# Rotary products and low parts of q and k on GpSimd alone, softmax row sums from four tiles on TensorE, first q and k in one transfer

## The chip, the core and the metric

One core of a Trainium2 chip runs the whole program. The metric is the device time of one execution in microseconds (us). Before the change it is 661.58 us, the median of 3 runs (661.09 to 662.1). Engines are named as in the profile: PE is TensorE (PEld its weight loads), DVE is VectorE, ACT is ScalarE, POOL is GpSimd, SP is SyncE, which issues nearly all transfers.

## What is computed

Four batches of eight heads, 576 positions, 64 features a head. q and k are rotated by position (RoPE), attended with a softmax, and the result goes through a soft mixture of 8 experts and then a wide squared-ReLU layer. All inputs are float32; matmuls run on float32 operands, some of them split in a rounded high part and a low part.

```python
q_rot, k_rot = rotate(q), rotate(k)          # x1*cos - x2*sin, x1*sin + x2*cos
scores = matmul(q_rot, k_rot.T) / 8
attn = exp(scores - max(scores))
attn = attn / (sum(attn) + 1e-9)
x = matmul(attn, v)                          # to (2304, 512)
logits = x @ phi                             # 32 slots
slot_in = softmax(logits, axis=0).T @ x
slot_out[e] = relu(slot_in[e] @ w1[e]) @ w2[e]
x = softmax(logits, axis=1) @ slot_out
out = (relu(x @ w_in) ** 2) @ w_out
```

## The kernel before

The 32 heads are worked off as 16 pairs of heads, numbered 0 to 15; the two heads of a pair stand on partitions 0 to 63 and 64 to 127. For a pair p these things happen:

- `load` (L303) brings k, q and their copies with swapped halves, 1.18 MB, into one of two buffers (`raws[p % 2]`), by three transfers. The buffer is free for pair p + 2 when the low parts of pair p have been computed.
- `rope_pair` (L321) rotates in place: for k (t = 0) and for q (t = 1) three operations on tiles of 128 x 576, times cosine, times sine, and the sum. All of them go through the helper `tt`, L317.
- `parts_pair` (L341): ACT rounds the rotated tile to its high part (`hi`, L347, three buffers), and `lo = a - hi` is a fourth operation a tile (L352, through L317 too; its rows read tL<-arena,tE). A `hi` buffer is free when the scores of the pair three before are done.
- `max_unit` (L379), ten times: PE forms scores from the high parts (L388), DVE takes the maximum over 576 columns in PSUM (L395). `max_rows` (L399) turns the maxima into a row (L406, L411, L416), and two small transfers (L421) bring it to where PE reads it. This runs 14 units ahead of the scores.
- `st_unit` (L431), ten units a pair (two halves of the queries, five tiles of keys): PE forms the transposed scores (L440, L444), ACT the exponentials (L453) into a tile P, and POOL adds the P of keys 0 to 3 into one tile `acc` (L461, three additions a half). The P tiles are a ring of six, with two more for the fifth.
- `pv_unit` (L466): PE multiplies P with v (L474).
- `norm` (L478), once a half: PE sums `acc` and the fifth P over the keys by a matmul with ones (L489, two groups of 64 columns at a time), DVE transposes (L493), inverts (L499, L500), transposes back (L504) and scales the result (L509). Then the pair's logits (L528, L533, L540).

The scores, maxima, row sums and a few others share a ring of three PSUM slots. After pair 15 come the experts, fed by weights from HBM, and then the wide layer on PE (L1345).

The order on each engine is not written by hand. Every step is given to `Plan.op` with the engines it may run on and their assumed costs, a due time, and the data it reads and writes; `Plan.emit` then lists the steps by a model of when each engine, slot and datum comes free, and an engine executes its list strictly in that order. The due times count in units, ten to a pair. Engines with a choice are written as a table, as in

```python
EITHER = {"POOL": 1.6, "DVE": 0.95}
on = {0: {"DVE": 0.8}, 1: {"POOL": 1.45}}.get(p, EITHER)
```

Transfers stand on SP in one list as well: the rows of maxima, v, the three of `load`, the expert weights.

## Time and profile before

| | |
|---|---|
| median of 3 runs | 661.58 us (661.09 to 662.1) |
| the profiled execution | 661.12 us, of which the trace spans 659.3 |
| mean granted TensorE clock | 0.968 |
| busy over the span: PE, DVE, ACT, POOL | 602.9, 438.4, 279.8, 256.3 us |
| last addition of logits (end of attention) | starts at 360.32 us |
| first matmul of L1345 on the chain (wide layer) | 425.79 us |

The span falls into three stages. Up to about 361 us the 16 pairs are worked off; POOL computes only here. From there to about 425 us the experts run while the weights stream in. From there to the end the wide layer keeps PE busy. A time in the rows below is counted from the span's start; "idle before" is the time an engine stood still before an instruction, and the name behind it is what ended that wait.

### The profile page before, as it was taken

The numbers are of one execution on the slowest core, as the hardware profiler recorded it, in microseconds if no ns is written. First come the engines' busy times: TensorE is split into PE (matmuls) and PEld (weight loads), VectorE is DVE, ScalarE is ACT, GpSimd is POOL, SyncE is SP. The second block draws the span as 40 slices with busy tenths as digits, with TensorE's granted clock in tenths as the row PEclk, the third lists the DMA queues.
The fourth block names the chain that finished last, engine by engine and source line by source line (L and its number), as shares of the span: only waits on it lengthen the run. The fifth ranks groups of instructions, "written<-read, shape, count | busy, mean of one in ns | idle before, by whom it ended". The sixth has DMA issues, their size and how long they took to land.

```text
span 659.3 us, 11254 instructions
## 1 busy us (share of the span) xinstructions
PE 602.9 (91%) x4437; PEld 408.2 (62%) x4437; DVE 438.4 (66%) x744; ACT 279.8 (42%) x492; POOL 256.3 (39%) x178
## 2 busy tenths in 40 slices
PE   2798998989889899899998988999999999999996
PEld 2555565546556555565665432677788788778885
DVE  2799867867776888776643543598569458455543
ACT  1142443434333444335443132479585446443440
POOL 1988988769666787666452000000000000000000
PEclk9688998998889999999999999999999999999999
DMA  8475534664365313402324999842130011000222
GB/s 183 95 169 157 152 106 121 157 156 128 93 157 156 83 30 76 93 21 85 136 79 157 390 387 389 338 127 82 47 128 1 0 65 64 1 1 0 96 95 96
DMA packets 36452, 80.76 MB, mean 122 GB/s; under 512 B 7632, under 2 KB 8048, under 8 KB 35440
## 3 DMA queue, kind: packets, MB, share of 16 engines
q1 hardware_dynamic: 35536, 79.16, 40.2%
q10 hardware_dynamic: 864, 0.89, 0.7%
q8 instruction: 35, 0.57, 0.4%
q14 instruction: 17, 0.14, 0.1%
HBM read 75.24 MB, written 4.72 MB: 121 GB/s over the span
## 4 chain that ended last, share of the span: by engine, by line
PE 55%; DMA 17%; DVE 9%; POOL 9%; issue 4%; SPq 3%; ACT 2%; DVEq 0%; POOLq 0%; ACTq 0%
PE bank L1345 30%; DMA arena<-in_qk_dram 13%; PE bank L474 5%; PE bank L440 4%; POOL arena L317 4%; DVE arena L317 4%; POOL pb L461 3%; PE bank L1277 2%; POOL tL L317 2%; PE bank L489 2%; SPq L309 2%; DVE mcol L395 2%; DMA pb<-in_w_in_dram 2%; PE bank L1071 2%; PE bank L1131 2%
## 5 line engine op out<-in xcount | busy, mean ns | idle before, releaser
L453 ACT ACTIVATE tO<-bank 128x576 f32<-128x576 f32 (+1 forms) x160 | 100.7, 648 | 187.5 <-PE bank L444 167.8
L1345 PE MATMUL bank<-w,tE 128*128 128x512 f32 x648 | 162.5, 399 | 1.1 <-ACT w__897 L1360 1.1
L1345 PEld LDWEIGHTS bank<-w,tE 128*128 128x128 f32 x648 | 120.6, 188 | 30.0 <-issue 2.9
L395 DVE TENSOR_REDUCE mcol<-bank 128x2 f32<-128x576 f32 x160 | 115.0, 745 | 34.3 <-PE bank L388 34.3
L474 PE MATMUL bank<-tO,pb 128*64 128x288 f32 x640 | 108.2, 436 | 2.6 <-DVE pb L509 2.4
L461 POOL TENSOR_TENSOR pb<-pb,tO 128x576 f32<-128x576 f32 x64 | 96.4, 1507 | 11.6 <-ACT tO L453 9.5
L317 POOL TENSOR_TENSOR arena<-arena 128x576 f32<-128x576 f32 x51 | 82.8, 1636 | 34.1 <-DMA arena<-in_qk_dram 30.2
L317 DVE TENSOR_TENSOR arena<-arena 128x576 f32<-128x576 f32 x45 | 64.3, 1444 | 21.2 <-DMA arena<-in_qk_dram 10.5
L440 PE MATMUL bank<-tE 64*128 64x288 f32 x320 | 60.5, 375 | 8.2 <-DVE mcol L395 6.2
L388 PE MATMUL bank<-tE 64*128 64x288 f32 x320 | 50.4, 352 | 17.4 <-DVE mrow L416 10.4
L461 POOL TENSOR_TENSOR pb<-tO 128x576 f32<-128x576 f32 x32 | 51.0, 1593 | 36.7 <-ACT tO L453 36.7
L440 PEld LDWEIGHTS bank<-tE 64*128 64x128 f32 x320 | 31.6, 194 | 46.3 <-issue 12.1
L474 PEld LDWEIGHTS bank<-tO,pb 128*64 128x64 f32 x640 | 35.5, 138 | 31.9 <-issue 17.4
L388 PEld LDWEIGHTS bank<-tE 64*128 64x128 f32 x320 | 29.9, 198 | 38.8 <-DVE mrow L416 12.9
L1345 PE MATMUL bank<-w,tO 128*128 128x512 f32 x216 | 52.7, 395 | 0.0
L440 PE MATMUL bank<-tL,tE 64*128 64x288 f32 x320 | 49.3, 305 | 0.0
L440 PE MATMUL bank<-tE,tL 64*128 64x288 f32 x320 | 49.2, 304 | 0.0
L444 PE MATMUL bank<-tE,pick 64*128 64x288 f32 x320 | 49.1, 303 | 0.0
L1345 PEld LDWEIGHTS bank<-w,tO 128*128 128x128 f32 x216 | 40.4, 188 | 8.8
L1288 ACT ACTIVATE pb<-bank 128x384 f32<-128x384 f32 x48 | 22.0, 493 | 49.5 <-PE bank L1277 36.1
L1288 ACT ACTIVATE arena<-bank 128x384 f32<-128x384 f32 x48 | 21.6, 489 | 35.1 <-PE bank L1277 33.4
L493 DVE STREAM_TRANSPOSE bank<-bank 128x288 f32<-128x288 f32 x32 | 15.8, 494 | 29.4 <-PE bank L489 29.4
(245 smaller groups left out, 840.1 us busy)
## 6 DMA issues: line engine op xcount, KB each, us to landing
arena<-in_qk_dram SPq DMA_DIRECT2D x15, 576.0 KB
arena<-in_qk_dram SPq DMA_DIRECT2D x15, 512.0 KB
pb<-in_v_dram SPq DMA_DIRECT2D x16, 320.0 KB
arena<-in_w_dram SPq DMA_DIRECT2D x8, 512.0 KB
tE<-in_w_dram SPq DMA_DIRECT2D x8, 512.0 KB
tL<-in_w_in_dram SPq DMA_DIRECT2D x3, 1024.0 KB
pb<-in_w_in_dram SPq DMA_DIRECT2D x3, 1024.0 KB
w__429<-in_w_dram SPq DMA_DIRECT2D x4, 512.0 KB
```

The lines of the kernel that those rows point to most:

```text
L309: lambda rows=rows, to=to, of=of, q=q: QUEUE[q].dma_start(out=raws[i][rows, ts_, to], in_=qk[p][rows, ts_, of]),
L317: ENG[e].tensor_tensor(out=o, in0=x, in1=y, op=how)
L388: nc.tensor.matmul(on_ring(tok)[:, j, 0:HQ], lhsT=hi[rows, 1, UNIT[u]], rhs=hi[rows, 0, HALF[h]], start=True, stop=True)
L395: lambda e: nc.vector.tensor_reduce(out=mcol[:, h, :, u], in_=on_ring(tok)[:, :, 0:HQ], op=ALU.max, axis=AX.X),
L440: nc.tensor.matmul(st[:, j, 0:HQ], lhsT=k[x][rows, UNIT[u]], rhs=q[y][rows, HALF[h]], start=(i == 0), stop=False)
L444: nc.tensor.matmul(st[:, j, 0:HQ], lhsT=pick[rows, :], rhs=mrow[rows, HALF[h]], start=False, stop=True)
L453: lambda e: nc.scalar.activation(out=pr[0:m], in_=on_ring(tok)[0:m, :, 0:HQ], func=AF.Exp, scale=0.125),
L461: lambda e: nc.gpsimd.tensor_tensor(out=acc, in0=one, in1=pr, op=ALU.add),
L474: nc.tensor.matmul(o_t[rows, 0:HQ], lhsT=vr[:, u, j, :], rhs=pr[:, j, :], start=(u == 0), stop=(u == 4))
L493: {"DVE": 0.47}, lambda e: nc.vector.transpose(out=on_ring(tok)[:, 1, 0:HQ], in_=on_ring(tok)[:, 0, 0:HQ]),
L1288: lambda e, i=i, h=h: nc.scalar.activation(out=rg_of()[:, 0, h], in_=BANKS[i][:, 0:384], func=AF.Relu),
L1345: nc.tensor.matmul(BANKS[PO[c]], lhsT=gt[:, x, 128 * c : 128 * c + 128], rhs=wo[:, fc % 2, y, :], start=(fc % FQ == 0 and i == 0), stop=(f ...
```

## The change

- `rope_pair`: all pairs but the first are rotated on POOL alone; before, pair 1 was, and the others could go to either engine.
- `parts_pair`: all low parts are formed on POOL alone; before, only those of pair 0.
- `st_unit`: POOL adds one pair of P tiles a half (keys 0 and 1), where it made three additions.
- `norm`: PE sums four things, `acc` and the P tiles of keys 2, 3 and 4, by eight matmuls of 32 columns of ones in four column groups; each group holds half of a head's sum. `inverse` gets four small additions (32 x 9) that add the partner group's half before the reciprocal.
- `first_loads`: the k and q of pair 0 come by one group of three transfers ahead of the tables, where two groups stood around the tables.
- the due times of the maxima of pair 1 are not below 0.1 + 0.4 n.

```diff
@@ rope_pair
-        on = {0: {"DVE": 0.8}, 1: {"POOL": 1.45}}.get(p, EITHER)
+        on = {"POOL": 1.45} if p else {"DVE": 0.8}
@@ parts_pair
-                EITHER if p else {"POOL": 1.45}, lambda e, a=a, hi=hi, lo=lo: tt(e, lo, a, f(hi), ALU.subtract), g + 2 * t + 1,
+                {"POOL": 1.45}, lambda e, a=a, hi=hi, lo=lo: tt(e, lo, a, f(hi), ALU.subtract), g + 2 * t + 1,
@@ st_unit
-        if 0 < u < 4:
-            one, k1 = p_slot(p, h, 0) if u == 1 else (acc, ak)
+        if u == 1:
+            one, k1 = p_slot(p, h, 0)
@@ norm
-        acc, (rest, rk) = accs[n], p_slot(p, h, 4)
+        acc, rest = accs[n], [p_slot(p, h, u) for u in (2, 3, 4)]
         tok = {}
+        QUAD = [slice(32 * i, 32 * i + 32) for i in range(4)]
 
         def sums(e):
             sm = on_ring(tok)[:, 0]
-            for i, x in enumerate((acc, rest)):
-                for j, rows in enumerate(HEADS):
-                    nc.tensor.matmul(sm[rows, 0:HQ], lhsT=ones, rhs=x[:, j, :], start=(i == 0), stop=(i == 1))
-
-        op({"PE": 1.1}, sums, g, [("acc", n), rk], [("sm", n)], take="ring", tok=tok, mode="c")
+            xs_ = [acc] + [x for x, _ in rest]
+            for i in range(2):
+                for j in range(2):
+                    for w in range(2):
+                        nc.tensor.matmul(
+                            sm[QUAD[2 * j + w], 0:HQ], lhsT=ones[:, 0:32], rhs=xs_[2 * i + w][:, j, :], start=(i == 0), stop=(i == 1)
+                        )
+
+        op({"PE": 1.15}, sums, g, [("acc", n)] + [k for _, k in rest], [("sm", n)], take="ring", tok=tok, mode="q")
@@ norm, inverse
             nc.vector.tensor_scalar(out=r9, in0=col, scalar1=1e-9, scalar2=None, op0=ALU.add)
+            for q in range(4):
+                nc.vector.tensor_tensor(out=r9[QUAD[q]], in0=r9[QUAD[q]], in1=col[QUAD[q ^ 1]], op=ALU.add)
             nc.vector.reciprocal(out=r9, in_=r9)
-        ring_op({"DVE": 0.39}, inverse, g, [("sm", n)], ["r9"], give="ring", tok=tok)
+        ring_op({"DVE": 0.9}, inverse, g, [("sm", n)], ["r9"], give="ring", tok=tok)
@@ first_loads
-        load(0, -99, slice(0, 4, 2), "ACT")
+        load(0, -99, slice(0, 4), "ACT")
...
-        load(0, -98.8, slice(1, 4, 2), "ACT")
@@ the loop over pairs
-            at(gm + n, max_unit, p, n // 2, n % 2, gm + n + (0.9 if n % 2 else 0.1))
+            at(gm + n, max_unit, p, n // 2, n % 2, max(gm + n + (0.9 if n % 2 else 0.1), 0.1 + 0.4 * n if p == 1 else -99))
```

The new lines shift the numbers: L474 stays, L489 becomes L492, L528 becomes L535.

Since the plan decides the order, three places of it follow, as the built programs have them.

POOL in the steady stretch, from the low parts of one pair to those of the next. Rows arena<-arena are rotary operations, tL<-arena,tE low parts, pb the additions of P tiles. Before, from the low parts of pair 12 to that of pair 13 (the other half of the operations stands on DVE):

```order
L317 TENSOR_TENSOR tL<-arena,tE 128x576 x2
L461 TENSOR_TENSOR pb<-tO_78 128x576
L461 TENSOR_TENSOR pb<-pb,tO_79 128x576 x2
L317 TENSOR_TENSOR arena<-arena 128x576 x2
L461 TENSOR_TENSOR pb<-tO_78 128x576
L317 TENSOR_TENSOR arena<-arena 128x576
L461 TENSOR_TENSOR pb<-pb,tO_78 128x576 x2
L317 TENSOR_TENSOR tL<-arena,tE 128x576
```

With the change, from the low parts of pair 13 to those of pair 14. The row "arena x2" is k of pair 15 times cosine and sine, whose data come by the load that waits for the low parts of pair 13; the addition after it is that of pair 11, second half:

```order
L317 TENSOR_TENSOR tL<-arena,tE 128x576 x2
L317 TENSOR_TENSOR arena<-arena 128x576
L461 TENSOR_TENSOR pb<-tO_79 128x576
L317 TENSOR_TENSOR arena<-arena 128x576 x2
L461 TENSOR_TENSOR pb<-tO_78 128x576
L317 TENSOR_TENSOR arena<-arena 128x576 x3
L317 TENSOR_TENSOR tL<-arena,tE 128x576 x2
```

All of the rotation now stands between one pair's low parts and the next's, and one addition stands behind the first two of its operations.

PE around the row sums of pair 11, second half, in pair 12. Before:

```order
L474 MATMUL bank_87<-tO_78,pb 64x288 x2
L489 MATMUL bank_86<-pb,ones 64x288 x2
L489 MATMUL bank_86<-tO_79,ones 64x288 x2
L388 MATMUL bank_85<-tE 128x288 x2
L440 MATMUL bank_84<-tE 128x288 x2
```

With the change:

```order
L474 MATMUL bank_87<-tO_78,pb 64x288 x2
L492 MATMUL bank_85<-pb,ones 32x288
L492 MATMUL bank_85<-tO_79,ones 32x288
L492 MATMUL bank_85<-pb,ones 32x288
L492 MATMUL bank_85<-tO_79,ones 32x288 x5
L388 MATMUL bank_84<-tE 128x288 x2
L440 MATMUL bank_86<-tE 128x288 x2
```

The sums stand at the same place among their neighbours, behind the fourth unit of pair 12, with eight narrow matmuls for four wide ones.

ACT at the start, where it issues transfers beside SP. Before:

```order
L309 DMA arena<-in_qk_dram 64x2x512
L309 DMA arena<-in_qk_dram 64x2x64
L818 DMA arena<-in_rope_dram 64x2x512
L818 DMA arena<-in_rope_dram 64x2x64
L309 DMA arena<-in_qk_dram 64x2x512
L309 DMA arena<-in_qk_dram 64x2x64
```

With the change:

```order
L309 DMA arena<-in_qk_dram 64x4x512
L309 DMA arena<-in_qk_dram 64x4x64
L825 DMA arena<-in_rope_dram 64x2x512
L825 DMA arena<-in_rope_dram 64x2x64
L347 ACTIVATE tE<-arena 128x576 x4
```

The second group behind the tables is gone; its bytes stand in the first.

## Rows read from the trace of the kernel before

**Rows 1.** The page, span in 40 equal slices: TensorE's granted clock in tenths of full speed

```profile
PEclk9688998998889999999999999999999999999999
```

**Rows 2.** Windows: steady stretch; one pair after the rotations end (us, busy PE, PEld, DVE, ACT, POOL, clock)

```profile
54.00:296.40 242.40, 220.84 (x2098) 137.42 (x2100) 189.61 (x322) 96.35 (x172) 187.65 (x121) 0.95 0.45 115
...
316.30:333.70 17.40, 17.40 (x180) 11.10 (x180) 11.06 (x24) 7.01 (x12) 8.50 (x6) 1.00 0.57 201
```

**Rows 3.** Waits of PE in 54 to 296 us: total us, times, longest

```profile
PE bank L388 <- DVE mrow L416: 10.4, 7, 3.0
PE bank L440 <- DVE mcol L395: 5.8, 6, 1.8
```

**Rows 4.** Groups of instructions: count, busy us, mean ns, idle before and its causes

```profile
L461 POOL TENSOR_TENSOR pb<-pb,tO 128x576 f32<-128x576 f32 x64 | 96.4, 1507 | 11.6 <-ACT tO L453 9.5
...
L317 POOL TENSOR_TENSOR arena<-arena 128x576 f32<-128x576 f32 x51 | 82.8, 1636 | 34.1 <-DMA arena<-in_qk_dram 30.2 <-DVE m L406 3.6
...
L317 DVE TENSOR_TENSOR arena<-arena 128x576 f32<-128x576 f32 x45 | 64.3, 1444 | 21.2 <-DMA arena<-in_qk_dram 10.5 <-DMA arena<-in_rope_dram 8.1 <-issue 2.5
...
L317 POOL TENSOR_TENSOR tL<-arena,tE 128x576 fp32r<-128x576 f32 x17 | 25.9, 1529 | 16.4 <-DMA arena<-in_qk_dram 14.3 <-ACT tE L347 1.9 <-PE bank L489 0.3
...
L317 DVE TENSOR_TENSOR tL<-arena,tE 128x576 fp32r<-128x576 f32 x15 | 20.6, 1378 | 2.3 <-ACT tE L347 2.3
```

**Rows 5.** Timeline of POOL (start, us, instruction): beside a DVE rotation; after the rotations

```profile
60.76 1.92 POOL L461 TENSOR_TENSOR pb<-pb,tO 128x576 f32<-128x576 f32 x1
...
321.51 1.41 POOL L461 TENSOR_TENSOR pb<-pb,tO 128x576 f32<-128x576 f32 x1 [0.20 <-ACT tO L453]
```

**Rows 6.** Timeline of POOL: low parts, then the first rotation on the next load

```profile
156.84 2.80 POOL L317 TENSOR_TENSOR tL<-arena,tE 128x576 fp32r<-128x576 f32 x2 [0.28 <-PE bank L489]
...
169.87 3.86 POOL L317 TENSOR_TENSOR arena<-arena 128x576 f32<-128x576 f32 x2 [4.99 <-DMA arena<-in_qk_dram]
...
243.23 2.79 POOL L317 TENSOR_TENSOR tL<-arena,tE 128x576 fp32r<-128x576 f32 x2
...
254.86 3.88 POOL L317 TENSOR_TENSOR arena<-arena 128x576 f32<-128x576 f32 x2 [3.64 <-DMA arena<-in_qk_dram]
...
265.20 1.41 POOL L317 TENSOR_TENSOR tL<-arena,tE 128x576 fp32r<-128x576 f32 x1
...
275.88 3.88 POOL L317 TENSOR_TENSOR arena<-arena 128x576 f32<-128x576 f32 x2 [4.18 <-DMA arena<-in_qk_dram]
```

**Rows 7.** The chain that ended last: the load is issued

```profile
266.64 0.55 SPq L309
```

**Rows 8.** Timelines at the start: DVE, POOL, PE

```profile
10.93 1.43 DVE L317 TENSOR_TENSOR arena<-arena 128x576 f32<-128x576 f32 x2 [8.08 <-DMA arena<-in_rope_dram]
14.83 2.89 DVE L317 TENSOR_TENSOR arena<-arena 128x576 f32<-128x576 f32 x4 [2.47 <-issue]
...
17.11 3.23 POOL L317 TENSOR_TENSOR tL<-arena,tE 128x576 fp32r<-128x576 f32 x2 [14.31 <-DMA arena<-in_qk_dram]
...
31.93 0.61 PE L440 MATMUL bank<-tE 64*128 64x288 f32 x2
```

**Rows 9.** Timeline of POOL: low part of pair 5

```profile
95.06 1.40 POOL L317 TENSOR_TENSOR tL<-arena,tE 128x576 fp32r<-128x576 f32 x1
```

**Rows 10.** Timelines: PE, sums of pair 11's second half; DVE, last logits

```profile
291.08 0.66 PE L489 MATMUL bank<-pb,ones 128*64 128x288 f32 x4
...
292.15 0.40 PE L388 MATMUL bank<-tE 64*128 64x288 f32 x2
...
360.32 0.35 DVE L540 TENSOR_TENSOR lg<-lg,bank 128x192 f32<-128x192 f32 x1 [0.70 <-PE bank L533]
```

**Rows 11.** Timeline of PE: matmuls in four groups of 32 columns; groups: a small DVE operation

```profile
363.13 1.42 PE L634 MATMUL bank<-x,es 128*32 128x512 f32 x16 [0.38 <-DVE es L601]
...
L499 DVE TENSOR_SCALAR r<-bank 128x9 f32<-128x9 f32 x32 | 4.8, 151 | 0.1
```

**Rows 12.** Windows: experts (us, busy PE, PEld, DVE, ACT, POOL, clock, DMA share, GB/s)

```profile
360.00:380.00 20.00, 18.46 (x153) 9.16 (x149) 9.82 (x42) 5.15 (x16) 0.53 (x1) 1.00 1.04 386
```

## The prediction

> **What bounds the kernel now.** I read the windows first. In the steady stretch of the 16 pairs, 54 to 296 us, PE is busy for 220.8 of 242.4 us, and the clock granted to it averages 0.95 [rows 2]; in slices up to 200 us it is below nine tenths of full speed, so part of them ran at 1.2 instead of 2.4 GHz, and after 200 us no slice is [rows 1]. The reader is to compare this with the second window: once the rotations are over, a whole pair takes 17.4 us with PE busy in all of it at full clock, while DVE and POOL do little [rows 2]. So PE has 21.6 us of idle time and 0.05 x 242.4 = 12.1 us of lost clock that are not its own work. The waits of PE say whose they are: the two rows on DVE (the row of maxima, and single maxima, that come late) hold 16.2 of the 21.6 us [rows 3]. DVE is late because its list holds rotations: 45 of them at 1.44 us and 15 low parts at 1.38 us, with idle time in front of them that transfers end [rows 4]. A rotation that waits for its data holds up every maximum listed behind it.
>
> I then followed POOL from pair to pair, because the change puts the rest there. The reader is to see a loop in it: low parts end, the freed buffer is loaded, POOL stands until the load has landed, rotates, and forms the next low parts. From the end of the low parts to the first rotation on the new data it takes 169.87 - 159.64 = 10.2, 254.86 - 246.02 = 8.8 and 275.88 - 266.61 = 9.3 us [rows 6]; SP issues the load 0.03 us after the low part ends [rows 7], so the rest is the transfer.
>
> **The change, part by part.**
>
> *DVE.* It loses 39 rotations (45 less the 6 of pair 0) and 15 low parts: 39 x 1.44 + 15 x 1.38 = 77 us, all of it ahead of maxima that PE waits for. It gains 4 x 32 small additions. No row shows one of 32 x 9; between nothing and the 151 ns of the nearest row, of 128 x 9 from PSUM [rows 11], I take 0.15, so 0.6 us a half and 19 us in all. DVE was busy for 189.6 of 242.4 us [rows 2] and will be for less, so this hides, but for the last half, where the end waits for it: +0.6 us.
>
> *POOL.* It loses 64 additions, 64 x 1.51 = 96 us, and gains 54 operations. What one costs depends on DVE: beside a DVE rotation 1.92 us, without one 1.41 us, although DVE then was busy with maxima, transposes and scaling for 11 of 17.4 us [rows 2, 5]. DVE keeps only operations of the second kind after pair 0, so I take 1.40 for each; the other end is 1.92.
>
> First the row, then two rules. POOL takes 1.4 us where a DVE rotation that meets no POOL operation takes 1.43 / 2 = 0.72 us [rows 5, 8]. The Trainium skill (GPSIMD Engine Reference, Engine selection) says elementwise work belongs on VectorE, since a two-input operation is about twice as slow on GpSimd. By that rule 54 moved operations cost 54 x (1.40 - 0.72) = 37 us of engine time, and the sum below would be some 37 us higher if POOL were the path throughout; by the rows POOL is on the path in part of the loop only. The Trainium skill (SBUF — State Buffer, Who interferes with whom) has a DVE operation with two SBUF inputs and a GpSimd operation that reads SBUF exclude each other for a whole instruction. That would make a contended one 1.40 + 0.72 = 2.1 us, and the trace has 1.92; with the change it leaves POOL uncontended.
>
> *The loop.* With the change a pass of it holds, behind the load, six operations (five rotations and one addition) and two low parts; the sixth rotation and the other addition run during the load. That is 9.3 + 8 x 1.40 = 20.5 us a pass, with 9.3 the middle of the three waits above. It is longer than PE's 17.4 us [rows 2], so **the loop, not PE, sets the pace** from pair 6 to 13. Of its eight passes (low parts of pair 5 to those of 13) the program's list has one with an operation less and one with one more: 6 x 20.5 + 19.1 + 21.9 = 164.0 us.
>
> *The start.* The first rotations wait for the tables until 10.93, the second group of pair 0 comes at 14.83, because it shares the queues with pair 1, and the six rotations end at 17.72 [rows 8]. In one transfer ahead of the tables, the whole of pair 0 has landed when the tables have. At about 10.9 six rotations of 0.72 end at 15.2: -2.5 us. Nothing gained, if the tables behind the larger transfer come at 13.4, is the other end; I take -2.5, as the bytes ahead of pair 1 are the same.
>
> *Up to pair 5.* POOL starts at 17.11 and ends the low part of pair 5 at 96.46 [rows 8, 9]. With the change it holds 51 operations there, 51 x 1.40 = 71 us, or 86 us from an earlier start of 14.6, if it never waits; it will wait for the loads of pairs 3 to 6, each of which follows the low parts by 9.3. I take the time of before less the start, 94.0, between 86 and 100.
>
> *PE.* The sums hold twice the instructions. Before, eight take 292.15 - 291.08 = 1.07 us, two groups at a time [rows 10]. If four groups run at a time, sixteen take the same; if only two do, 1 us more. Sixteen of mostly 512 columns in four groups take 1.42 us [rows 11], which only fits four at a time. I take +0.1 for the narrower steps and the change of grouping beside the P x v matmuls; before the end nine sums lie on the path: +0.9 us. In the loop's stretch PE waits anyway.
>
> *The sum.* The low parts of pair 13 end at 94.0 + 164.0 = 258.0. The load takes 9.3; two rotations and the second addition of pair 11 end 4.2 later, at 271.5. The sums of that half are listed behind the fourth unit of pair 12 and need that addition. Before, they started at 291.08 [rows 10]. So 271.5 - 291.1 = -19.6 us, and from there to the last logits at 360.32 [rows 10] the work is PE's as before. With +0.9 and +0.6: -18.1 us. The experts run under transfers at 386 GB/s [rows 12] that start as attention's buffers come free, and the wide layer follows; both move with it. 661.1 - 18.1 = **643 us** against the profiled execution's 661.12, which is 0.46 below the median of 661.58.
>
> What is late next: PE before the row sums, on POOL's addition, and then ACT, which must write the high parts of a pair in its list's order and has the exponentials queued behind them.
>
> **The rivals.**
>
> *PE bounds throughout.* If loads land sooner (SP issues them earlier, nothing else being late) the loop has slack, and all of PE's idle time and clock come back: 21.6 + 12.1 + 2.5 - 1.5 = 34.7 us, **626 us**. For it: the window at 17.4 us a pair. Against: none of the three waits is under 8.8 us, and even that gives 20.0 a pass.
>
> *The loop is longer.* With the longest wait seen, 10.2, nine waits make it 8 us later, and the early passes up to 4: **651 to 655 us**. For it: the expert weights load in the same stretch. Still faster.
>
> *POOL stays contended and the change loses.* Between the low parts of pair 5 and the sums of pair 11's second half stand 67 POOL operations on the path. At 1.92 instead of 1.40 they take 35 us more: **678 us**. The point from which it decides: 18.1 / 67 = 0.27, so at a mean over 1.67 us the change is slower. For it: the mean of POOL's rotations now is 1.64 [rows 4], just below. Against: that mean comes with DVE rotations, and the additions after these end take 1.41 [rows 5].
>
> *The wait only changes its name.* The loop now runs at 20.6 us (266.61 - 246.02) [rows 6]. If PE waits for POOL in the end as long as it did for DVE, the time is **660 to 662**. Against: it would need the slack that the loop already shows against PE's end to vanish.
>
> **How the numbers follow.** The forecast has 0.61, the longer loop 0.20, PE as the bound 0.09, the same time 0.03, the contended POOL 0.07. A measurement of this kernel tells about 0.2% from no change. Faster is 0.61 + 0.20 + 0.09 = 0.90, same 0.03, slower 0.07. The forecast's own bounds are a wait of 8.8 (nine of them: -4.5) and pair 5 at 86 (-8) on one side, pair 5 at 100 (+6) and no gain at the start (+2.5) on the other, which seldom fall together: 634 to 651. With the longer loop the range goes to 655; PE as the bound, the same time and the contended POOL are left out (0.19): 634 to 655.
>
> **What would show it.** POOL's rotations at a mean near 1.40 us, and no DVE rows of L317 but six. First score matmul at about 28 to 29.5 instead of 31.93. Low parts of pair 13 near 258. PE's waits: the row of maxima nearly gone, in its place the row sums (L492) on POOL's addition, or ACT's high parts on POOL. The span between the sums of pair 11 and the last logits stays about 69 us. It is wrong if POOL's mean stays over 1.6, if DVE still ends PE's longest waits, if sixteen narrow matmuls take over 1.5 us, or if PE is busy all through 150 to 270 us.

## The result, and the profile after

The changed kernel takes 641.92 us (median of 4 runs, 641.52 to 642.19) beside 661.84 us for the kernel before on the same chip: a ratio of 0.9687, with a 95% interval of 0.965 to 0.9725. It is faster. 643 had been forecast, and the range of 634 to 655 holds the time. The profiled execution took 642.19 us and spans 640.4.

The sum came out within 2 us, but the way it was reached did not. The signs that the prediction named separate the two, so I take them first from the profile.

The page of the kernel after, costliest groups (line, engine, operation, count | busy us, mean ns of one | idle time just before them and what ended it); they answer to [rows 4]:

```profile
L317 POOL TENSOR_TENSOR arena<-arena 128x576 f32<-128x576 f32 x90 | 125.4, 1414 | 56.3 <-DMA arena<-in_qk_dram 56.0
L461 POOL TENSOR_TENSOR pb<-tO 128x576 f32<-128x576 f32 x32 | 45.2, 1413 | 39.6 <-ACT tO L453 39.6
L317 POOL TENSOR_TENSOR tL<-arena,tE 128x576 fp32r<-128x576 f32 x32 | 45.2, 1427 | 20.6 <-ACT tE L347 20.6
L506 DVE TENSOR_TENSOR r<-r,bank 32x9 f32<-32x9 f32 x128 | 20.7, 162 | 2.4
```

POOL's operations take 1.41 to 1.43 us, as forecast, where rotations took 1.64 before. The small additions take 0.162 us (0.15 was assumed).

The windows of both kernels over equal work, from the logits of pair 0 to those of pair 12. The columns are the stretch, its length, the busy time of PE, of its weight loads, of DVE, ACT and POOL (with instruction counts), the granted clock, and the share and rate of the DMA engines. First the kernel before:

```profile
65.21:316.25 251.04, 229.74 (x2192) 141.64 (x2192) 192.46 (x334) 101.99 (x187) 188.40 (x122) 0.96 0.42 106
```

and the kernel after, with its last stretch to the last logits behind it:

```profile
63.14:295.17 232.03, 221.93 (x2384) 132.38 (x2384) 153.24 (x387) 101.34 (x188) 164.66 (x120) 1.00 0.47 120
295.17:342.06 46.89, 42.69 (x474) 26.07 (x473) 23.25 (x71) 16.99 (x30) 7.29 (x7) 0.99 0.36 127
```

The twelve pairs are 251.04 - 232.03 = 19.0 us shorter. PE's idle time falls from 251.04 - 229.74 = 21.3 to 10.1 us, which gives 11.2; the other 7.8 us is PE's busy time, which shrinks although PE now has more instructions, because the granted clock rises from 0.96 to 1.00. Behind pair 12 it goes the other way: 46.89 us to the last logits, where before it took 360.32 - 316.25 = 44.1 us.

The waits of PE from 30 to 345 us (operation <- what released it: us in total, times, longest), which answer to [rows 3]:

```profile
PE bank L474 <- DVE pb L516: 11.0, 23, 0.6
PE bank L535 <- DVE pb L516: 2.7, 1, 2.7
PE bank L474 <- DMA pb<-in_v_dram: 0.9, 1, 0.9
PE bank L492 <- DVE mcol L395: 0.7, 1, 0.7
```

The waits for the row of maxima and for single maxima, 16.2 us before, are gone. In their place is one of half a microsecond, 23 times in the 32 halves: P x v (L474) waits for the scaling on DVE (L516). There is no row at all in which PE waits for POOL. That contradicts the step of the prediction in which POOL's loop sets the pace.

Two timelines show that wait. The first is DVE in the kernel after, behind the row sums of one half (start, us, instruction, idle before it):

```profile
244.10 0.50 DVE L498 STREAM_TRANSPOSE bank<-bank 128x288 f32<-128x288 f32 x1 [1.08 <-PE bank L492]
244.51 0.72 DVE L395 TENSOR_REDUCE mcol<-bank 128x2 f32<-128x576 f32 x1
245.15 0.15 DVE L504 TENSOR_SCALAR r<-bank 128x9 f32<-128x9 f32 x1
245.34 0.69 DVE L506 TENSOR_TENSOR r<-r,bank 32x9 f32<-32x9 f32 x4
246.06 0.21 DVE L507 RECIPROCAL r<-r 128x9 f32<-128x9 f32 x1
246.31 0.48 DVE L511 STREAM_TRANSPOSE pb<-r 128x288 f32<-128x288 f32 x1
246.89 0.46 DVE L516 TENSOR_TENSOR pb<-bank,pb 128x288 f32<-128x288 f32 x1
```

The second is PE in the same stretch:

```profile
246.51 0.42 PE L388 MATMUL bank<-tE 64*128 64x288 f32 x4
247.41 0.71 PE L474 MATMUL bank<-tO,pb 128*64 128x288 f32 x4 [0.48 <-DVE pb L516]
```

The four small additions stand in this chain with 246.06 - 245.34 = 0.72 us. PE runs out of other work 0.48 us before the chain ends.

POOL in the same kernel, over one pass of its loop:

```profile
251.79 2.78 POOL L317 TENSOR_TENSOR tL<-arena,tE 128x576 fp32r<-128x576 f32 x2
254.54 1.39 POOL L317 TENSOR_TENSOR arena<-arena 128x576 f32<-128x576 f32 x1
255.90 1.41 POOL L461 TENSOR_TENSOR pb<-tO 128x576 f32<-128x576 f32 x1
262.80 2.79 POOL L317 TENSOR_TENSOR arena<-arena 128x576 f32<-128x576 f32 x2 [5.49 <-DMA arena<-in_qk_dram]
265.55 1.40 POOL L461 TENSOR_TENSOR pb<-tO 128x576 f32<-128x576 f32 x1
266.91 4.17 POOL L317 TENSOR_TENSOR arena<-arena 128x576 f32<-128x576 f32 x3
271.04 2.77 POOL L317 TENSOR_TENSOR tL<-arena,tE 128x576 fp32r<-128x576 f32 x2
```

The low parts of pair 13 end at 254.57 (258.0 was forecast), and the addition that pair 11's second row sums need ends at 266.95. Those sums start 1.9 us later:

```profile
268.89 0.43 PE L492 MATMUL bank<-pb,ones 128*32 128x288 f32 x1
```

This pass takes 271.04 - 251.79 = 19.3 us. The eight passes from pair 5 (its low parts end at 93.81) to pair 13 take (254.57 - 93.81) / 8 = 20.1 us in the mean, and PE's pairs over the same stretch (313.99 - 160.40) / 8 = 19.2, from logits to logits. So the loop is even the longer of the two, and yet PE does not wait for it, because POOL starts with a lead. Its addition for the second half of pair 4 is this one:

```profile
124.80 1.42 POOL L461 TENSOR_TENSOR pb<-tO 128x576 f32<-128x576 f32 x1
```

It ends 9.4 us before the sums that need it, which start at 135.66. For the second halves of pairs 7, 9 and 11 the lead is 4.6, 3.5 and 1.9 us. The rotations are over before it is used up.

### The profile page after: what moved, and what is told of

It reads as the page before. It is cut to its first block, busy times and chain, and to the rows that moved or that the text cites. A ratio compares the mean times of both kernels' runs of the same rounds, so it can differ in the third digit from the quotient of the medians.

```text
span 640.4 us, 11744 instructions
## 1 busy us (share of the span) xinstructions
PE 593.0 (93%) x4689; PEld 396.3 (62%) x4689; DVE 386.6 (60%) x818; ACT 278.6 (43%) x492; POOL 215.6 (34%) x168
## 4 chain that ended last, share of the span: by engine, by line
PE 76%; DVE 14%; DMA 5%; issue 2%; ACT 2%; SPq 1%; DVEq 0%; ACTq 0%
PE bank L1351 31%; PE bank L474 11%; PE bank L440 9%; PE bank L492 6%; DVE mcol L395 4%; PE bank L388 3%; PE bank L1283 3%; DVE r L506 2%; DMA pb<-in_w_in_dram 2%; PE bank L444 2%; DMA arena<-in_rope_dram 2%; PE bank L1077 2%; DVE pb L516 2%; PE bank L558 2%; DVE pb L511 2%
## 5 line engine op out<-in xcount | busy, mean ns | idle before, releaser
L317 POOL TENSOR_TENSOR arena<-arena 128x576 f32<-128x576 f32 x90 | 125.4, 1414 | 56.3 <-DMA arena<-in_qk_dram 56.0
L474 PE MATMUL bank<-tO,pb 128*64 128x288 f32 x640 | 105.0, 426 | 11.9 <-DVE pb L516 11.0
L474 PEld LDWEIGHTS bank<-tO,pb 128*64 128x64 f32 x640 | 34.9, 135 | 42.1 <-DVE pb L516 16.3
L461 POOL TENSOR_TENSOR pb<-tO 128x576 f32<-128x576 f32 x32 | 45.2, 1413 | 39.6 <-ACT tO L453 39.6
L440 PE MATMUL bank<-tE 64*128 64x288 f32 x320 | 56.7, 351 | 0.1
L317 POOL TENSOR_TENSOR tL<-arena,tE 128x576 fp32r<-128x576 f32 x32 | 45.2, 1427 | 20.6 <-ACT tE L347 20.6
L388 PE MATMUL bank<-tE 64*128 64x288 f32 x320 | 49.3, 341 | 2.5 <-DVE mcol L395 1.6
L440 PEld LDWEIGHTS bank<-tE 64*128 64x128 f32 x320 | 30.1, 185 | 31.6 <-issue 21.3
L440 PE MATMUL bank<-tL,tE 64*128 64x288 f32 x320 | 47.2, 292 | 0.0
L444 PE MATMUL bank<-tE,pick 64*128 64x288 f32 x320 | 47.2, 291 | 0.0
L440 PE MATMUL bank<-tE,tL 64*128 64x288 f32 x320 | 47.2, 291 | 0.0
L388 PEld LDWEIGHTS bank<-tE 64*128 64x128 f32 x320 | 28.6, 188 | 24.4 <-issue 10.8
L492 PE MATMUL bank<-tO,ones 128*32 128x288 f32 x384 | 37.5, 410 | 0.0
```

Of the source, the lines that this page charges most:

```text
L317: ENG[e].tensor_tensor(out=o, in0=x, in1=y, op=how)
L388: nc.tensor.matmul(on_ring(tok)[:, j, 0:HQ], lhsT=hi[rows, 1, UNIT[u]], rhs=hi[rows, 0, HALF[h]], start=True, stop=True)
L440: nc.tensor.matmul(st[:, j, 0:HQ], lhsT=k[x][rows, UNIT[u]], rhs=q[y][rows, HALF[h]], start=(i == 0), stop=False)
L444: nc.tensor.matmul(st[:, j, 0:HQ], lhsT=pick[rows, :], rhs=mrow[rows, HALF[h]], start=False, stop=True)
L461: lambda e: nc.gpsimd.tensor_tensor(out=acc, in0=one, in1=pr, op=ALU.add),
L474: nc.tensor.matmul(o_t[rows, 0:HQ], lhsT=vr[:, u, j, :], rhs=pr[:, j, :], start=(u == 0), stop=(u == 4))
```

## The experiments

The theories, as the expectations name them. **A** is the prediction's: POOL's loop sets the pace. **B**: PE and the DVE chain behind its row sums do, with POOL's loop about 2 us behind. **C**: as B, but the loop has all the slack it needs. The second batch gave rise to **D**, on what exactly PE waits for. The kernel before measured 661.1 to 664.9 us in these batches, so kernels of different batches are compared through their ratios to it.

| run | median us | ratio to before | 95% interval |
|---|---|---|---|
| the change | 641.92 | 0.9687 | 0.965 to 0.9725 |
| small additions left out | 638.94 | 0.9661 | 0.9619 to 0.9702 |
| POOL's addition left out | 641.18 | 0.9694 | 0.9658 to 0.9731 |
| both left out | 628.24 | 0.9496 | 0.9453 to 0.954 |
| rotations on either engine again | 669.16 | 1.0129 | 1.0062 to 1.0196 |
| old row sums | 639.74 | 0.9689 | 0.9651 to 0.9726 |
| first q and k in two groups | 640.11 | 0.9692 | 0.9653 to 0.9731 |
| row sums earlier | 645.51 | 0.9774 | 0.9735 to 0.9813 |
| row sums earlier, load split | 646.36 | 0.9794 | 0.9748 to 0.9839 |
| row sums earlier, two output tiles | 634.14 | 0.9547 | 0.9494 to 0.9601 |
| the same, load split | 638.29 | 0.9596 | 0.9556 to 0.9636 |
| row sums earlier, two output tiles, first q and k in two groups | 631.13 | 0.952 | 0.9502 to 0.9538 |
| two output tiles alone | 638.72 | 0.9637 | 0.9618 to 0.9656 |

### Who sets the pace: two additions, each left out, and both

The first edit takes the small additions out of the chain:

```diff
             nc.vector.tensor_scalar(out=r9, in0=col, scalar1=1e-9, scalar2=None, op0=ALU.add)
-            for q in range(4):
-                nc.vector.tensor_tensor(out=r9[QUAD[q]], in0=r9[QUAD[q]], in1=col[QUAD[q ^ 1]], op=ALU.add)
             nc.vector.reciprocal(out=r9, in_=r9)
```

> The four small additions of each half (32 x 9, between the row sums and the reciprocal) are left out, their place in the lists kept; each row sum then holds half of its terms. Theory A, the prediction's (POOL's loop of load, rotations and low parts sets the pace, the small additions hide behind it but for the last half): 641.9 - 0.6 = 641.3, between 640.5 and 642. Theory B (PE sets the pace, and the chain on DVE after the row sums holds up the first P x v of every half by some 0.5 us; POOL's loop stands only about 2 us behind): from pair 0 to 11 the loop takes over after 2 us are gained, and the 9 halves behind it give 9 x 0.5: 641.9 - 2 - 4.5 = 635.4, between 633 and 637. Theory C (as B, but POOL's loop has all the slack it needs): 32 x 0.5 = 16 us less, 626, between 624 and 629.

The second takes the addition off POOL:

```diff
-                lambda e: nc.gpsimd.tensor_tensor(out=acc, in0=one, in1=pr, op=ALU.add),
+                lambda e: None,
...
-            xs_ = [acc] + [x for x, _ in rest]
+            xs_ = [rest[0][0]] + [x for x, _ in rest]
```

> POOL's addition of the first two tiles of each half (32 x 1.40 us) is left out, the lists else the same; the row sums take the third tile twice in its place, so the sums lack two of five tiles. Theory A (POOL's loop sets the pace): a pass loses 2 x 1.4 = 2.8 us, over the eight passes 22 us, until PE bounds: 620 to 627. Theories B and C (PE and the chain behind its row sums set the pace): the two additions a pass were not on the path, 641 to 642.

The third has both edits.

> Both left out: the small additions on DVE and POOL's addition of two tiles, so the row sums lack most of their terms. Theory A: as without POOL's addition alone, 620 to 627, and no more than 1 us below that run. Theory B: POOL's loop falls to about 17.5 us a pass and stands behind no longer, so all 32 halves give their 0.5 us: 625 to 628, some 8 to 10 us below the run without the small additions alone. Theory C: the same as without the small additions alone, within 1 us.

Measured: 641.18 without POOL's addition (A wanted 620 to 627), 638.94 without the small additions, and 628.24 without either; B's ranges for these two end 2 us and 0.2 us lower. Leaving the small additions out gives 0.26% of the time of before while POOL has its additions (within the intervals), and 0.9694 - 0.9496 = 2.0%, or 13 us, once POOL has none. Such a pair of numbers is what two limits close to each other look like: either one, removed alone, uncovers the other.

**A falls.** Without its additions POOL only stands longer. The waits of POOL in that run, from 54 to 272 us, where the kernel after has 54.5 us for the same transfers:

```profile
POOL arena L317 <- DMA arena<-in_qk_dram: 74.0, 12, 9.7
```

B's second half also shows, by a path that no theory had named. In the run without the small additions the waits of PE from 30 to 345 us begin:

```profile
PE bank L444 <- DMA tE<-mrow: 6.5, 3, 3.6
```

PE waits for the row of maxima, that is for a transfer of 3 KB. SyncE's queue in the same run says why:

```profile
154.39 1.87 SPq L309 DMA_DIRECT2D arena<-in_qk_dram  x3
156.30 1.07 SPq L802 DMA_DIRECT2D w__1594<-in_w_dram  x2
157.47 1.50 SPq L421 DMA_DIRECT2D tE<-mrow  x2
```

The load of a pair (L309) is issued when POOL's low parts end, at 154.36. The expert weights and then the row stand behind it in the list. The row is issued at 157.47 and PE can use it at 166.18, after the 1.18 MB of the load and 1 MB of weights ahead of it. So a late low part on POOL reaches PE through the queue, and PE does not need to wait for POOL itself. With POOL's additions left out as well, that load is issued at 150.04 and the row at 156.74, and no such wait is left in PE's list.

The same place shows what such a pause costs besides its length. Windows of that run, with the columns as above:

```profile
162.00:166.10 4.10, 0.59 (x8) 0.36 (x6) 1.89 (x5) 0.00 (x0) 2.27 (x2) 0.91 0.72 232
166.10:168.00 1.90, 1.82 (x8) 1.09 (x10) 0.00 (x0) 0.65 (x1) 1.90 (x3) 0.50 0.00 0
168.00:170.00 2.00, 2.00 (x14) 1.14 (x12) 0.46 (x1) 0.00 (x0) 2.00 (x2) 0.50 0.00 0
170.00:172.00 2.00, 2.00 (x14) 0.86 (x10) 1.31 (x2) 0.65 (x1) 2.00 (x3) 0.50 0.56 164
172.00:174.00 2.00, 2.00 (x22) 1.46 (x22) 0.57 (x2) 1.07 (x2) 2.00 (x3) 0.94 0.00 0
```

PE did 0.59 us of work in 4.1 us, and for the next 6 us it was granted 0.50 of full speed, that is 1.2 GHz. Six microseconds at half speed are three lost. The pair took 24.35 us from logits to logits where the next took 17.72, 6.6 us more for a wait of 3.58.

### Which part of the change made the gain

Rotations and low parts may go to either engine again; all the rest stays as after the change.

```diff
-        on = {"POOL": 1.45} if p else {"DVE": 0.8}
+        on = EITHER if p > 1 else {"POOL": 1.45} if p else {"DVE": 0.8}
...
-                {"POOL": 1.45}, lambda e, a=a, hi=hi, lo=lo: tt(e, lo, a, f(hi), ALU.subtract), g + 2 * t + 1,
+                EITHER if p else {"POOL": 1.45}, lambda e, a=a, hi=hi, lo=lo: tt(e, lo, a, f(hi), ALU.subtract), g + 2 * t + 1,
```

> Only the rotations and low parts go back to a choice of DVE or POOL (42 rotations from pair 1 on and 2 low parts then stand on DVE, 44 operations of 54 in the kernel before); row sums, first transfers and the due time of the maxima stay as after the change. All theories that put the gain down to DVE, freed of rotations ahead of the maxima: the wait of PE for the row of maxima and for single maxima comes back by about 44 of 54 parts, 16.2 x 44 / 54 = 13 us, part of the lost clock with it: 650 to 660. A theory that puts it down to POOL's 64 additions alone: POOL has still less to do than after the change, so 642 or less.

Measured: 669.16, a ratio of 1.0129. That is 1.3% above the kernel before (interval 0.6 to 2.0%), and 9 us above the upper end of what was expected. The groups of that run:

```profile
L317 POOL TENSOR_TENSOR arena<-arena 128x576 f32<-128x576 f32 x48 | 80.0, 1681 | 73.1 <-DMA arena<-in_qk_dram 72.7
L317 DVE TENSOR_TENSOR arena<-arena 128x576 f32<-128x576 f32 x48 | 68.2, 1437 | 16.1 <-DMA arena<-in_qk_dram 15.8
L461 POOL TENSOR_TENSOR pb<-tO 128x576 f32<-128x576 f32 x32 | 51.4, 1606 | 69.9 <-ACT tO L453 69.9
```

and its waits of PE from 30 to 270 us:

```profile
PE bank L440 <- DVE mcol L395: 10.8, 15, 1.8
PE bank L474 <- DVE pb L516: 7.0, 15, 0.5
PE bank L388 <- DVE mrow L416: 4.2, 6, 1.6
```

The waits for maxima are back (15.0 us), and the wait on the chain behind the sums comes on top (7.0). POOL's operations are contended again, up to 1.68 us. A POOL with less to do is worth nothing here: it stands idle while PE waits for DVE.

The other way round, only the row sums go back: three additions on POOL, two groups of columns, no small additions.

```diff
-        if u == 1:
-            one, k1 = p_slot(p, h, 0)
+        if 0 < u < 4:
+            one, k1 = p_slot(p, h, 0) if u == 1 else (acc, ak)
...
-            xs_ = [acc] + [x for x, _ in rest]
-            for i in range(2):
-                for j in range(2):
-                    for w in range(2):
-                        nc.tensor.matmul(
-                            sm[QUAD[2 * j + w], 0:HQ], lhsT=ones[:, 0:32], rhs=xs_[2 * i + w][:, j, :], start=(i == 0), stop=(i == 1)
-                        )
+            for i, x in enumerate((acc, rest)):
+                for j, rows in enumerate(HEADS):
+                    nc.tensor.matmul(sm[rows, 0:HQ], lhsT=ones, rhs=x[:, j, :], start=(i == 0), stop=(i == 1))
...
-            for q in range(4):
-                nc.vector.tensor_tensor(out=r9[QUAD[q]], in0=r9[QUAD[q]], in1=col[QUAD[q ^ 1]], op=ALU.add)
```

> Only the row sums go back to the kernel before (three additions a half on POOL, sums in two groups of 64 columns, no small additions); rotations and low parts stay on POOL, first transfers and due times as after the change. POOL then has 186 - 32 + 32 = 218 operations of 1.4 us in place of 154, 64 x 1.41 = 90 us more, and in the list the additions stand between the rotations. A theory in which POOL is on the path in this kernel: a pass of its loop grows by four additions, of which those beside the load wait cost nothing: 2 to 4 x 1.4 = 2.8 to 5.6 us on 20.0, 22.8 to 25.6 us against PE's 18.0; some 12 passes, less the 2 us of lead: 641.9 + 12 x (4 to 7) = 690 to 720, slower than before the change. A theory in which POOL has slack and only DVE's freed list made the gain: 630 to 642.

Measured: 639.74, a ratio of 0.9689 beside the change's 0.9687. **The gain comes from the rotations and low parts that leave DVE; the new row sums change nothing that these runs can tell.** The due times of pair 1's maxima were not varied alone; they stand in this run and in the slower one above, so they do not make the gain by themselves. The expectation that leaned on POOL missed by 50 us. The window of that run from the logits of pair 0 to those of pair 12 shows what it had overlooked:

```profile
62.68:294.71 232.03, 225.26 (x2198) 137.13 (x2198) 138.84 (x292) 102.88 (x187) 231.50 (x170) 1.00 0.48 120
```

POOL is busy for 231.50 of 232.03 us. The additions that this kernel lists between the rotations fill the time in which POOL otherwise stands for the load. A pass is therefore not the load wait plus the operations behind it. Here a pair's 14 operations fill 232.03 / 12 = 19.3 us; after the change a pass of ten operations with the wait uncovered takes 20.1. That is nearly the same pace with a full engine as with one that stands idle for a quarter of the time (163.2 us busy of 218 after the change, from 54 to 272 us).

Then the start alone: the first q and k come in two groups again, with the tables between.

```diff
-        load(0, -99, slice(0, 4), "ACT")
+        load(0, -99, slice(0, 4, 2), "ACT")
...
+        load(0, -98.8, slice(1, 4, 2), "ACT")
         dma(lambda: nc.sync.dma_start(out=ident, in_=ident_in), -98.7, 65, (), ["ident"])
```

> Only the first q and k come again in two groups, with the tables between, as before the change; nothing else moves on PE, DVE or POOL. The prediction's step (one transfer gives the first rotations 2.5 us): 641.9 + 2.5 = 644.4. What the two traces show (first rotation at 15.8 in place of 10.9 us, first scores 1.3 us later after the change): 641.9 - 1.3 = 640.6. If the loss at the start is taken up behind it (PE's work to pair 0 ended earlier all the same): 641.5 to 642.3.

Measured: 640.11; the ratios, 0.9692 and 0.9687, do not separate the two. The traces do. DVE's rotations of pair 0 in the kernel after:

```profile
15.80 4.22 DVE L317 TENSOR_TENSOR arena<-arena 128x576 f32<-128x576 f32 x6 [12.95 <-DMA arena<-in_rope_dram]
```

and with two groups:

```profile
10.93 1.43 DVE L317 TENSOR_TENSOR arena<-arena 128x576 f32<-128x576 f32 x2 [8.08 <-DMA arena<-in_rope_dram]
14.91 2.89 DVE L317 TENSOR_TENSOR arena<-arena 128x576 f32<-128x576 f32 x4 [2.56 <-issue]
```

With one transfer the tables are there at 15.8 in place of 10.9 us. In the kernel after, SyncE issues the load of pair 1 at 2.74 us; with two groups it issues it at 6.26. The DMA engines have no room in that stretch (their mean busy share in the kernel after is 0.92 or more in every 2 us from 2 to 14 us), so the tables share them with that load. The first transfer ahead of the tables is larger too, and the runs do not separate the two. The first scores start at 33.23 with one transfer and at 28.62 with two, the last logits at 342.06 and 338.53. By these two executions, this part of the change costs some 3.5 us of attention, and the span shrinks by 2.9 when it is undone.

### What PE waits for behind the row sums

If the wait is for the bank that the scaling reads, then listing the row sums earlier gives the chain time to end. One number is changed:

```diff
-    norm=4.2, rope=-22.0, parts=-20.0, v=-5.0, lag=2.5, mr0=0.0, lgt=5.5, slots=6.0,
+    norm=2.7, rope=-22.0, parts=-20.0, v=-5.0, lag=2.5, mr0=0.0, lgt=5.5, slots=6.0,
```

> One number is changed after the change: the row sums are due 1.5 units earlier, so that PE's list has two units and more between the sums of a half and the first P x v that needs the bank which the scaling on DVE reads. Nothing is left out. Theory B (PE waits on the chain behind the sums, POOL's loop stands 2 us behind): the 0.5 us a half go from PE's waits, but the loop takes over, as in the run without the small additions: 638 to 640. Theory C (the loop has slack): 626 to 629. Theory A (the loop sets the pace already): 641 to 643.

The next run also splits the load of a pair:

```diff
-            at(g0 - 39.8, load, p, g0 - 37, slice(0, 4))
+            at(g0 - 39.8, load, p, g0 - 37, slice(2, 4))
+            at(g0 - 39.75, load, p, g0 - 36.9, slice(0, 2))
```

> The row sums due 1.5 units earlier, and the load of a pair split in two: the copies with swapped halves, whose buffer is free once the rotation's addition has run, are listed ahead of the plain q and k, whose buffer waits for the low parts. Nothing is left out. Theory B: with half of the load ahead of the low parts, POOL waits some 4 us less a pass (16 in place of 20 us), so the loop falls behind PE, and PE's waits on the chain are gone as well: 627 to 631, near the run with both additions left out (628.2). Theory C: the same as the earlier sums alone, within 1 us. If the split's three more issues on SP and its waits hold up the rows of maxima listed behind: 632 to 642.

Measured: 645.51 and 646.36, both slower than the change. The split changed nothing beyond a microsecond, as C had it, but none of the theories had the earlier sums slower. PE's wait had not gone but grown. From 30 to 345 us the run with the earlier sums has:

```profile
PE bank L474 <- DVE pb L516: 12.9, 28, 0.7
```

In total that is 1.9 us more than after the change, which is only a part of the loss; the rest stays open. By the lists, every P x v that waits now fills the bank of the other half, which the scaling does not read. What the two banks share is the tile: both output banks were declared as one tile of two banks (name bank, number 3). If the waits are laid between instructions that touch the same tile, every first P x v listed behind a scaling waits for it, whichever bank it fills. That is theory D, and its edit is one declaration:

```diff
-    PAIRS = [psum.tile([128, 2, 512], F32, name=f"bank{i}") for i in range(4)]
-    BANKS = [PAIRS[i // 2][:, i % 2] for i in range(8)]
+    PAIRS = [psum.tile([128, 2, 512], F32, name=f"bank{i}") for i in range(3)]
+    BANKS = [PAIRS[i // 2][:, i % 2] for i in range(6)] + [psum.tile([128, 512], F32, name=f"obank{i}")[:, :] for i in range(2)]
```

> As the run with the earlier row sums, and the two output banks that P x v fills (one for each half) are declared as two tiles of one bank in place of one tile of two. Nothing is left out. Theory D (what holds the first P x v behind the scaling is not the bank but the tile that holds both: every P x v listed behind the scaling of either half waits, so listing the sums earlier could not help): PE's wait at L474 on the scaling, 12.9 us in 28 times, is gone, and with it as much as the additions' run showed if POOL's loop takes over (637 to 640), or all of it if the loop has slack (627 to 633). If the wait is on the bank itself: 645, as the run with the earlier sums alone.

> As the run before it (earlier sums, two tiles for the output banks), with the load of a pair split in two, the swapped copies ahead. Nothing is left out. If POOL's loop bounds once PE's wait on the scaling is gone: the split shortens its pass by some 4 us, 627 to 631, 7 us or more below the run without the split. If the loop has slack then: the same as without the split, within 1.5 us. If the wait is on the bank itself: 645 to 647 as before.

> After the change, only the output banks are declared as two tiles; the sums keep their due time, and nothing is left out. Theory D (the tile that holds both banks makes every first P x v behind a scaling wait): the wait goes where the P x v behind the scaling fills the other half's bank, and stays where it fills the same bank, which by the lists is once a pair: PE's 18 waits at L474 fall to about 9, 641.9 - 16 x 0.48 = 634.2 at most, and if POOL's loop takes over before, 637 to 640. If the wait is on the bank itself: 641 to 643.

Measured with the earlier sums: 634.14, a ratio of 0.9547 against 0.9774 without the two tiles. The wait of L474 on L516 is gone from PE's waits, and the window from the logits of pair 0 to those of pair 12 has PE busy for 223.5 of 225.0 us:

```profile
61.53:286.55 225.02, 223.49 (x2384) 133.80 (x2384) 154.38 (x387) 102.06 (x188) 166.17 (x121) 1.00 0.49 124
```

D holds. The time lies between the two ranges that D had named, 627 to 633 and 637 to 640: PE waits for POOL's addition (L492 on L461) once, for 0.4 us, so the loop is now close to its limit. Split loads made this worse (638.29), which no expectation had: the split run's waits of PE show POOL's addition behind the rotations that the earlier half of a load lets go ahead of it in the list,

```profile
PE bank L492 <- POOL pb L461: 5.7, 4, 2.5
```

so the run does not tell whether a shorter loop alone would have helped.

The two tiles alone, with the sums at their old place, gave 638.72 (0.9637). Of 18 waits at L474 from 30 to 270 us, nine were expected to stay; three did:

```profile
PE obank L474 <- DVE pb L516: 1.2, 3, 0.4
```

Why the other six went as well is open. The time is nevertheless about that of the run without the small additions (638.94), for the same reason: at 166.20 PE has waited 1.9 us for the row of maxima, and the clock falls behind it (0.51 from 168 to 170 us). With the earlier sums the low parts of that pair end at 150.80 in place of 154.54, and SyncE issues the load at 150.82 in place of 154.57. The row follows at 156.85 in place of 158.52, so 6.0 us behind the load and not 4.0, and PE does not wait for it.

### A version that is faster than both

Earlier sums, two tiles for the output banks, and the first q and k in two groups, over the changed kernel:

> As the run with earlier sums and two tiles for the output banks, and the first q and k again in two groups as before the change. Nothing is left out. The first transfers alone gave 1.8 us in the total and 3.5 us at the last logits when undone after the change: 634.1 - 1.8 = 632.3, between 630 and 634. If PE's list, saturated here, had taken up the late start already: 634 to 635.

Measured: 631.13 (630.18 to 632.04), a ratio of 0.952 with an interval of 0.9502 to 0.9538, against 0.9687 for the change. The last logits come at 328.57, 4.1 us earlier than with one first transfer (332.68). The totals of these two runs are not separated: their intervals overlap.

## Why the prediction was right, and where it was not

**The total.** 643 was forecast, -18.1 us against the profiled execution; it became 642.19, -18.9. Last logits were forecast at 360.32 - 18.1 = 342.2 and come at 342.06. This was in part luck, because errors of 2 to 4 us cancel. The first scores came 3.8 us behind the forecast, and yet the low parts of pair 5 ended at 93.81 (94.0 forecast). The eight passes took 160.8 us for 164.0. The sums of pair 11's second half started at 268.89 for 271.5, 2.6 early, and from there to the last logits it took 2.5 longer than allowed.

**Right: DVE's list was the cause.** The prediction put PE's waits and lost clock down to rotations in front of maxima on DVE. They go with the rotations (clock 0.96 to 1.00, 16.2 us of waits gone) and come back with them (669.16).

**Right: POOL uncontended.** 1.40 was taken, 1.41 to 1.43 measured, so the rival in which it stays contended fell. The run with shared rotations has 1.68 for the same operation. The Trainium skill (GPSIMD Engine Reference, Engine selection) would have elementwise work on VectorE, as about twice as slow on GpSimd. The duration agrees (1.41 beside the 4.22 / 6 = 0.70 us of pair 0's rotations on DVE), but as advice for this kernel it is contradicted: with 48 rotations on DVE the ratio is 1.0129, with 6 it is 0.9687.

**Right: four groups of 32 columns run side by side.** The sums of one half in the kernel after, first instruction, and the instruction behind them:

```profile
242.79 0.43 PE L492 MATMUL bank<-pb,ones 128*32 128x288 f32 x1
243.90 0.40 PE L388 MATMUL bank<-tE 64*128 64x288 f32 x2
```

Sixteen matmul rows take 1.11 us where eight took 1.07 [rows 10].

**Wrong: "the loop, not PE, sets the pace".** No wait of PE on POOL is in the trace, and without POOL's additions the time stays (641.18). The loop term was close in size (20.1 us a pass against 20.5 forecast), and the loop was indeed longer than PE's pair. What the prediction left out is POOL's lead: 9.4 us at pair 4, of which 1.9 was left at pair 11, so PE never had to wait. And PE's pair was not the 17.4 us of [rows 2]: it took 18.8, 20.4 with the work on slots, and 0.95 us of the 18.8 are the wait for the scaling, which the prediction did not have. Two limits within 2 us of each other let the wrong one give the right sum.

**Wrong: "this hides, but for the last half".** The 19 us of small additions were set against DVE's busy share, which falls. But they stand in a chain that PE's next P x v waits for. Their 0.72 us a half put about 0.4 us on PE's path: (641.18 - 628.24) / 32, in the runs without POOL's additions. The prediction costed an engine's load where it should have followed one result.

**Wrong: the start.** -2.5 was taken, with "nothing gained" as the other end; the first scores came 1.3 us later than before, at 33.23. The step failed at "the bytes ahead of pair 1 are the same": pair 1's load is issued at 2.74 in place of 6.10 us and shares the DMA engines with the tables, which came at 15.8, later than the 13.4 of that other end. A loss had been excluded without a reason.

**Wrong: from there "the work is PE's as before".** From the sums of pair 11's second half to the last logits 70.7 us were allowed (69.2 + 0.9 + 0.6), and it took 342.06 - 268.89 = 73.2. PE's idle time there grew from 2.6 to 5.1 us. P x v waits 2.5 us for the scaling where it waited 0.6, and the last logits, which stand at the end of the chain, wait 2.7 where before it was

```profile
PE bank L528 <- DVE pb L509: 1.8, 1, 1.8
```

The +0.6 for the end was thus near (+0.9); the waits of P x v had no term. PE's own work grew by 1.4 us, where +0.9 was allowed.

**The rivals.** PE bounds throughout: nearly so in what it does, but at 18.8 us a pair, not at 17.4. The run with both additions left out reaches 628.24, close to the 626 that this rival named. The longer loop did not come: 20.1 us a pass, where its wait of 10.2 gives 10.2 + 11.2 = 21.4. In part the wait did only change its name: 11.0 us of PE's waits now stand before P x v, but they are on DVE's scaling and not on POOL.

## What to carry to other kernels

When work moves off a shared engine, ask of each small operation that the move adds which single result it delays and who needs that result next; a low busy share of its engine does not hide it. A loop over an engine that waits for transfers has no fixed length per operation, since work listed into the wait is free until the engine is full; and a loop that is longer than the engine it feeds costs nothing while its lead lasts. The waits between PE and DVE were here on what is declared as one object: before the order around such a wait is tuned, check whether the waiting instruction touches the same data or only the same tile.

## What the runs showed of the hardware that was not expected

A 3 KB transfer issued behind 2.2 MB on the same queue was usable 8.7 us after its issue (157.47 to 166.18). A PE that had done 0.59 us of work in 4.1 us then ran at 1.2 GHz for about 6 us, which nearly doubled the cost of the 3.58 us wait. And POOL's two-input operations over 576 columns take 1.41 us beside DVE's maxima, transposes and scaling; what slows them are two-input operations of that size on DVE. In the kernel before, the 72 POOL operations that overlap with a rotation or low part on DVE take 1.76 us in the mean and up to 2.01, the other 92 take 1.41. The slowing goes both ways: those DVE operations take 1.49 us in the mean beside POOL's and 0.75 alone.
